# Seven block products for eight in the second pair of batches

## The chip, the cores and the metric

One core of a Trainium2 chip. The time is device microseconds of one execution; before the change the median of 3 runs is 703.04 us (702.79 to 703.9). The profile is of one further execution.

## The reference

Causal attention over 4 batches, 12 heads, 448 tokens, head dimension 64, then a gated product with no nonlinearity. Cut to what matters:

```python
scores = np.where(mask, -1e9, q @ k.T / 8)             # 4 x 12 x 448 x 448
attn = exp(scores - max) / (sum + 1e-9) @ v
x = attn laid out as (4 * 448) x 768
return ((x @ w_a) * (x @ w_b)) @ w_out                  # w_a, w_b: 768 x 1536, w_out: 1536 x 768
```

## The kernel before

Everything is held with features on the 128 partitions and the 448 tokens of one batch along the row. A weight unit is 128 output columns of a matrix with 768 input rows: 12 units of w_a ("a"), 12 of w_b ("b"), and 12 of w_out ("o", six output tiles, each in two halves of the 1536 inputs). One matmul takes 128 x 128 weights and 128 x 448 moving values into one PSUM bank; 6 k-tiles make a unit. Each fp32 operand is split into a high part, rounded to the format fp32r by a copy on ACT, and a low part, the rest, by a subtraction on DVE; a k-tile is three matmuls, hi by hi, hi by lo and lo by hi (`products`, L514). So a unit and batch is a group of 18 matmuls in one bank, and three banks "m" take turns.

The weights come as 64-bit words. DVE and ACT turn each unit into fp32 once (`convert_unit`, L297), and it is kept in HBM (`w_keep`).

The work has two passes over the same weights. Pass 1 takes batches 0 and 1, pass 2 batches 2 and 3. A pass is a list (`order`, L496): f = 0 to 5 with a then b, then six o units of the first half; f = 6 to 11, then six o units of the second half. `uses` (L549) walks it: for an a unit ACT copies the bank to SBUF ("mid"); for a b unit DVE multiplies bank and copy to g, and `part_g` splits g (g_hi by ACT, g_lo by DVE); an o unit reads g, and its first half goes to HBM (`o_keep`) and is added to the second. `split_unit` (L335) splits the weights of a unit ("w_hi", "w_lo", three buffers each).

The attention of batches 0 and 1 runs first. That of batches 2 and 3 is strewn into pass 1: `attend` (L594) counts k-tiles, and every 34 (`AT`) it puts in one pair of heads: scores, then in the next round the transposes and the product with v. The result x is stored in HBM (`x_keep`), and in the last six units of pass 1 `take_x` (L488) loads and splits it, 12 tiles, into the rooms that x of batches 0 and 1 has left.

All this only records operations with an engine, a cost and what they read and write. `Plan.order` (L125) then lists them: of the operations whose inputs are ready by its costs it takes the next for each engine, by age with some patience. The engines run what it wrote in that order, and semaphores hold an instruction until its inputs are there. Every DMA of the two passes is issued by SP, in one queue.

Of the kernel before, what the change touches and what calls it, by code (L numbers as in the profile page):

```python
# [9 lines left out]
F32 = mybir.dt.float32  # L10
# [31 lines left out]

AT = (2, 34)
STEP = (8, 3, 8)

PACE = (0, 0, 0, 0, 0, 0, 0, 0, 1, 0, 1, 0, 0)
LEAD = (2, 1)
# [170 lines left out]
def causal_attention_then_gated_product(  # L218
# [15 lines left out]
    def sb(tag, n, shape, dt=F32):  # L234
        return plan.ring(tag, n, lambda i: sbuf.tile(shape, dt, tag=f"{tag}{i}", name=f"{tag}{i}"))
# [13 lines left out]
    mask = const.tile([P, S], F32, name="mask")  # L249
    p_buf = [const.tile([P, PW], F32, name=f"p{i}") for i in range(NPB)]  # L250
    sm_buf = [const.tile([P, 2, 4], F32, name=f"sm{i}") for i in range(2)]
# [32 lines left out]

    w_64, w_32, w_parts = [], [], []

    def load_words(u):
# [3 lines left out]

    def load_kept(u):
        t = sb("w_32", 3, [P, UW])
        load(P * UW * 4, lambda: t.t, lambda: w_keep[u], [("keep", u)], [t])
        w_32.append(t)

    def convert_unit():  # L297
# [28 lines left out]
        w_32.append(wt)  # L326

    def split_unit():
        t = w_32.pop(0)
        hi, lo = sb("w_hi", 3, [P, KT, P], F32R), sb("w_lo", 3, [P, KT, P], F32R)  # L330

        def flat(x):
            return x.t.rearrange("p k f -> p (k f)")

        copy("act", UW, lambda: flat(hi), lambda: t.t, [t], [hi])  # L335
        two_input("dve", UW, lambda: flat(lo), lambda: t.t,
                  lambda: flat(hi).bitcast(F32), ALU.subtract, [t, hi], [lo])
        w_parts.append((hi, lo))


    qk, v_of, p_of, pt = {}, {}, {}, {}
    nth = [0, 0]

# [152 lines left out]
    order = []  # L496
    for _ in range(2):
# [4 lines left out]
    in_turn = [place[kind](n) for kind, n in order]  # L502
    xs, a_sb = {}, {}
# [9 lines left out]

    def products(ps, parts, k, hi, lo, first, last, keys):  # L514
        def mm():
            for n, (a, x) in enumerate(((parts[0], hi), (parts[0], lo), (parts[1], hi))):
                r = nc.tensor.matmul(  # L517
                    ps.t[:, :S], a.t[:, k, :], x(), start=first and n == 0, stop=last and n == 2
                )
            return r  # L520

        plan.op("pe", 3 * 203, mm, [parts[0], parts[1], *keys], [ps])

# [9 lines left out]
    def convert_next():  # L533
        n = turned[0]
        turned[0] += 1
        if n < NU:
            plan.soonest = HOLD[0] + HOLD[1] * n if n <= LEAD[0] else 0.0
            convert_unit()
            plan.soonest = 0.0
            load_next()  # L540
        elif n < len(in_turn):
            load_kept(in_turn[n])

    def split_next():
        if parted[0] < len(in_turn):
            split_unit()
        parted[0] += 1

    def uses():  # L549

        for n, (kind, f) in enumerate(order):
            first = n // NU * 2
            if n == NU - ET:
                for b in range(2, B):
                    xs[b] = x_parts()
            if NU - ET <= n < NU:
                for b in range(2, B):
                    take_x(b, xs[b], n - (NU - ET))
            convert_next()
            parts = w_parts.pop(0)  # L560
            split_next()
            for b in range(first, first + 2):
# [5 lines left out]
                for k in range(KT):  # L568
                    if kind == "o":
                        products(ps, parts, k, lambda k=k, b=b: g_hi[:, b % 2, k, :], lambda k=k, b=b: g_lo[:, b % 2, k, :],  # L570
                                 k == 0, k == KT - 1, [("g_hi", b % 2, k), ("g_lo", b % 2, k)])
                    else:
                        x_hi, x_lo = xs[b]
                        products(ps, parts, k, lambda k=k, x=x_hi: x.t[:, k, :], lambda k=k, x=x_lo: x.t[:, k, :],
                                 k == 0, k == KT - 1, [(x_hi, k), (x_lo, k)])
                    if k == KT - 1:
# [5 lines left out]
                        elif kind == "b":  # L582
                            two_input("dve", S, lambda t=t: t.t, lambda ps=ps: ps.t[:, :S],
                                      lambda a=a_sb[b]: a.t, ALU.mult, [ps, a_sb[b]], [t])
                            part_g(b, f, lambda t=t: t.t, t)
                        else:
                            two_input("dve", S, lambda t=t: t.t, lambda ps=ps: ps.t[:, :S],
                                      lambda a=acc: a.t, ALU.add, [ps, acc], [t])
                        if kind == "o":
# [112 lines left out]
```

## Time and profile before

| | us |
|---|---|
| median of 3 runs | 703.04 |
| profiled execution | 702.95 |
| its span, first to last instruction | 701.2 |
| PE busy | 690.3 |
| DVE busy | 391.3 |
| ACT busy | 341.6 |

The span has three parts: the attention of batches 0 and 1, up to some 102 us; pass 1 with the attention of batches 2 and 3, up to 438.1; pass 2, up to 697.3; then the last eviction and store. A busy time is the sum of instruction lengths with overlaps taken once. Matmuls overlap, so what one costs is read from the distance of two starts, and the same holds for DVE and ACT instructions where the queue is full.

### The profile page before, as it was taken

What the parts mean: (1) busy time and instruction counts of PE and PEld (TensorE: products, weight loads), DVE (VectorE), ACT (ScalarE), POOL (GpSimd) and SP (SyncE); (2) the same over time, 40 slices, a digit from 0 to 9 for tenths busy, and PEclk for the clock granted to TensorE, in tenths of its full rate; (3) what the DMA queues carried; (4) which work ended last, traced back from release to release, by engine and by line L of the source; (5) the groups of instructions that cost most, each with busy time, mean ns of one, the idle gap of its engine ahead of it and who ended that gap; (6) DMA issues with size and microseconds to landing.
All of it is one profiled execution on the core that took longest, in us unless ns stands there. A gap on an engine that the chain in (4) does not pass through costs nothing.

```text
span 701.2 us, 10638 instructions
## 1 busy us (share of the span) xinstructions
PE 690.3 (98%) x3884; PEld 598.8 (85%) x3884; DVE 391.3 (56%) x933; ACT 341.6 (49%) x817; POOL 56.2 (8%) x107
## 2 busy tenths in 40 slices
PE   8999999999999999999999999999999999999997
PEld 6665568898898898898898888999999999999997
DVE  6899998988876765777856543322331113322421
ACT  5778757667666667567566453222222222222100
POOL 4455650000000000000000000000000000000000
PEclk9999999999999999999999999999999999999999
DMA  8325535666655665443311566211214322121342
GB/s 313 117 86 164 147 120 175 228 195 224 205 206 188 224 218 182 153 154 145 141 66 51 189 195 190 63 65 46 67 46 148 122 87 67 45 68 46 97 133 92
DMA packets 41716, 95.85 MB, mean 137 GB/s; under 512 B 4800, under 2 KB 27840, under 8 KB 41664
## 3 DMA queue, kind: packets, MB, share of 16 engines
q1 hardware_dynamic: 41664, 95.18, 40.7%
q8 instruction: 30, 0.49, 0.3%
q14 instruction: 22, 0.18, 0.1%
HBM read 67.24 MB, written 27.92 MB: 136 GB/s over the span
## 4 chain that ended last, share of the span: by engine, by line
PE 90%; ACT 3%; DVE 3%; POOL 2%; DMA 1%; issue 1%; SPq 0%; POOLq 0%; ACTq 0%
PE m L517 74%; PE t L447 6%; PE s L379 5%; PE pv L467 4%; ACT p L398 2%; POOL p L425 2%; DVE p L392 1%; DMA raw<-kT 1%; ACT pt L263 1%; DVE rc L412 1%; PE m L379 1%; DVE pt L271 1%; SPq L282 0%; DVE w_m L312 0%; DVE rc L415 0%
## 5 line engine op out<-in xcount | busy, mean ns | idle before, releaser
L517 PE MATMUL m<-x_hi,w_hi 128*128 128x448 f32 x576 | 212.8, 369 | 0.0
L517 PE MATMUL m<-x_lo,w_hi 128*128 128x448 f32 x576 | 209.1, 363 | 0.0
L517 PE MATMUL m<-x_hi,w_lo 128*128 128x448 f32 x576 | 207.6, 360 | 0.0
L279 DVE TENSOR_TENSOR w_lo<-w,w_hi 128x768 fp32r<-128x768 f32 x72 | 69.0, 958 | 142.9 <-ACT w_hi L263 134.7
L517 PEld LDWEIGHTS m<-x_hi,w_hi 128*128 128x128 f32 x576 | 108.1, 188 | 11.3 <-issue 2.7
L398 ACT ACTIVATE p<-p,nm 128x448 f32<-128x448 f32 (+1 forms) x192 | 95.2, 498 | 43.0 <-DVE nm L392 42.8
L517 PEld LDWEIGHTS m<-x_hi,w_lo 128*128 128x128 f32 x576 | 107.7, 187 | 7.6
L517 PEld LDWEIGHTS m<-x_lo,w_hi 128*128 128x128 f32 x576 | 108.2, 188 | 5.3
L517 PE MATMUL m<-g_hi,w_hi 128*128 128x448 f32 x288 | 106.0, 368 | 0.0
L517 PE MATMUL m<-g_lo,w_hi 128*128 128x448 f32 x288 | 104.5, 363 | 0.0
L517 PE MATMUL m<-g_hi,w_lo 128*128 128x448 f32 x288 | 103.8, 360 | 0.0
L263 ACT ACTIVATE mid<-m 128x448 f32<-128x448 f32 x72 | 39.0, 541 | 123.5 <-PE m L517 112.9
L263 ACT ACTIVATE w_hi<-w 128x768 fp32r<-128x768 f32 x72 | 60.5, 840 | 55.2 <-PE m L517 54.9
L447 PE MATMUL t<-ident,p 128*128 128x128 f32 x384 | 64.4, 277 | 4.3 <-ACT pt L263 2.9
L392 DVE CUSTOM_DVE_ANT_0 p<-s,mask 128x448 f32<-128x448 f32 (+3 forms) x144 | 53.0, 414 | 25.7 <-PE s L379 25.6
L447 PEld LDWEIGHTS t<-ident,p 128*128 128x128 f32 x384 | 46.5, 140 | 14.1 <-POOL p L425 6.0
L517 PEld LDWEIGHTS m<-g_hi,w_hi 128*128 128x128 f32 x288 | 54.1, 188 | 5.0 <-issue 0.7
L517 PEld LDWEIGHTS m<-g_hi,w_lo 128*128 128x128 f32 x288 | 53.9, 187 | 3.9
L425 POOL TENSOR_SCALAR p<-p,rc 128x320 f32<-128x320 f32 (+2 forms) x96 | 53.2, 571 | 43.2 <-ACT p L398 26.1
L517 PEld LDWEIGHTS m<-g_lo,w_hi 128*128 128x128 f32 x288 | 54.1, 188 | 2.6
L263 ACT ACTIVATE pt<-t 128x512 f32<-128x512 f32 x72 | 41.2, 594 | 30.0 <-PE t L447 29.7
L279 DVE TENSOR_TENSOR mid<-m,mid 128x448 f32<-128x448 f32 x48 | 29.9, 624 | 46.4 <-PE m L517 46.1
(48 smaller groups left out, 655.6 us busy)
## 6 DMA issues: line engine op xcount, KB each, us to landing
w<-w SPq DMA_DIRECT2D x36, 768.0 KB, 4.5
w_keep<-w SPq DMA_DIRECT2D x36, 384.0 KB, 3.1
w<-w_keep SPq DMA_DIRECT2D x36, 384.0 KB, 3.0
raw<-qT SPq DMA_DIRECT2D x24, 224.0 KB, 2.7
raw<-kT SPq DMA_DIRECT2D x24, 224.0 KB, 3.1
o_keep<-mid SPq DMA_DIRECT2D x24, 224.0 KB, 1.9
acc<-o_keep SPq DMA_DIRECT2D x24, 224.0 KB, 2.7
out<-mid SPq DMA_DIRECT2D x24, 224.0 KB, 1.9
```

The costliest lines, as they stand in the source:

```text
L263: return nc.scalar.activation(o(), i(), AF.Copy)
L271: return nc.vector.tensor_copy(o(), i())
L279: plan.op(engine, ns, lambda: e.tensor_tensor(out=o(), in0=a(), in1=b(), op=op), reads, writes)
L379: r = nc.tensor.matmul(banks[j].t[:, at[i]], q[:, QS[i]:QS[i] + P], k[:, 0:QE[i]], start=True, stop=True)
L392: return nc.vector.tensor_tensor_reduce(out=chunk(p, i), in0=bk.t[:r, at[i]], in1=m, scale=-0.125, scalar=3.0e38, op0=ALU.add, op1=ALU.min ...
L398: return nc.scalar.activation(chunk(p, i), chunk(p, i), AF.Exp, bias=nm.t[:r, j, i:i + 1], scale=-1.0, accum_out=sm.t[:r, j, i:i + 1],)
L412: plan.op("dve", 69 + n, lambda sj=sj, si=si: nc.vector.tensor_scalar_add(rc.t[:, sj, si], sm.t[:, sj, si], 1.0e-9), [(sm, j, i) for j in ...
L425: return nc.gpsimd.tensor_scalar(out=pc, in0=pc, scalar1=s, scalar2=1.0, op0=ALU.mult, op1=ALU.mult)
L447: return nc.tensor.matmul(t.t[:, at:at + P], p.t[:, PO[i] + 128 * c:PO[i] + 128 * (c + 1)], swapped if swap else ident, is_transpose=True, ...
L467: r = nc.tensor.matmul(ps.t[j * D:(j + 1) * D, 128 * c:S], vt.t[:, c, j, :], parts[j, n].t[:, o:o + S - 128 * c], start=c == 0, stop=c == 3,)
L517: r = nc.tensor.matmul(ps.t[:, :S], a.t[:, k, :], x(), start=first and n == 0, stop=last and n == 2)
```

## The change

In pass 2 the two batches, x of batch 2 beside x of batch 3, and the two halves of the 768 inputs make a 2 x 2 of blocks B11, B12 (batch 3), B21, B22. For each f the a unit and the b unit are the two rows of a 2 x 2 of weight blocks, 384 x 128 each. The product of the two was 8 block products (4 groups of 18 matmuls); it is now 7 block products of 9 matmuls by Strassen's scheme in Winograd's form. An entry "s" takes the place of a and b in the list. The o units and pass 1 compute what they did.

- Weights: `prepare_all` makes S1 = b1 + b2, S2 = S1 - a1, S3 = a1 - b1, S4 = a2 - S2 on DVE (384 columns each), and splits the seven blocks one by one, four ahead of their use. `w_hi` and `w_lo` are one tile each of six half units.
- x: `take_first` and `take_second` load the 12 tiles, make T1 to T4 by 12 subtractions of 448 columns on DVE, and split the seven blocks, 21 splits. They begin five units before the end of pass 1. B11, B21, T1 and B22 lie in the old rooms of x, T2, T3 and T4 in buffers of the attention (p, pt) and of the 64-bit words (w_64).
- Products: `seven` runs them over three banks in the order B11 in bank A, T2 in B, B21 added in A, T3 added in B, T1 in C, T4 added in B, B22 added in C. ACT copies bank A after B11 (s1) and after B21 (c11). DVE adds s1 or an earlier sum to bank B or C after T2 (u2), T3 (u3), T1 (c22), T4 (c21) and B22 (c12); then c21 times c11 and c12 times c22 are g.
- `AT` is 30 instead of 34, so that the attention's rooms are free earlier.

```diff
-AT = (2, 34)
+AT = (2, 30)
+AHEAD = 4
+    w_hi = const.tile([P, 18, P], F32R, name="w_hi")
+    w_lo = const.tile([P, 18, P], F32R, name="w_lo")
...
+    def split(n, src, key, halves):
+        i = 3 * halves[0].tile
+        hi, lo = (x[:, i:i + n // P, :].rearrange("p k f -> p (k f)") for x in (w_hi, w_lo))
+        copy("act", n, lambda: hi, src, [key], [(h, 0) for h in halves])
+        two_input("dve", n, lambda: lo, src, lambda: hi.bitcast(F32), ALU.subtract,
+                  [key, *((h, 0) for h in halves)], [(h, 1) for h in halves])
...
-    def take_x(b, x, k):
-        t = sb("acc", 3, [P, S])
-        load(P * S * 4, lambda: t.t, lambda: x_keep[b - 2][k], [("xk", b, k)], [t])
-        split_x(x, k, lambda: t.t, t, False)
+    def take_first(k):
+        one, two = (sb("raw", 4, [P, 2, S]) for _ in range(2))
...
+        for t, i, b, kk in ((one, 0, 2, k), (one, 1, 3, k), (two, 1, 3, k + 3), (two, 0, 2, k + 3)):
+            load(P * S * 4, lambda t=t, i=i: t.t[:, i], lambda b=b, kk=kk: x_keep[b - 2][kk], [("xk", b, kk)], [(t, i)])
+        split_block("B11", k, b11, (one, 0))
+        both(b11, b12, b11, ALU.subtract, [(one, 1)], [(one, 0)])
+        split_block("T1", k, b11, (one, 0))
+        both(b12, b22, b12, ALU.subtract, [(two, 1)], [(one, 1)])
+        split_block("B22", k, b22, (two, 1))
+        both(b22, b22, b11, ALU.subtract, [(one, 0)], [(two, 1)])
+        split_block("T2", k, b22, (two, 1))
+        split_block("B21", k, b21, (two, 0))
+    def take_second(k):
+        one, two = raw_x[k]
+        split_block("T3", k, lambda: one.t[:, 1], (one, 1))
+        both(lambda: two.t[:, 0], lambda: two.t[:, 0], lambda: two.t[:, 1], ALU.subtract, [(two, 1)], [(two, 0)])
+        split_block("T4", k, lambda: two.t[:, 0], (two, 0))
...
-            order += [("ab"[r], f) for f in range(h * HF, (h + 1) * HF) for r in range(2)]
+            for f in range(h * HF, (h + 1) * HF):
+                order += [("a", f), ("b", f)] if r == 0 else [("s", f)]
...
+    def prepare_all(f0):
+        for f in range(f0, f0 + HF):
+            a, b = weights[f]
+            for i in range(7):
+                if i in (0, 4):
+                    if f + 1 < f0 + HF:
+                        weights.setdefault(f + 1, []).append(load_32(place["ab"[i // 4]](f + 1)))
...
+                if i == 1:
+                    sub(s12, lower, b, lower, b, upper, ALU.add)
+                    sub(s12, upper, s12, lower, a, lower)
+                if i == 3:
+                    sub(s34, lower, a, lower, b, lower)
+                    sub(s34, upper, a, upper, s12, upper)
+                t, at = ((a, lower), (s12, upper), (a, upper), (s34, lower), (s12, lower), (b, upper), (s34, upper))[i]
+                h = half()
+                split(384, lambda t=t, at=at: t.t[:, at], t if t in (a, b) else (t, at.start), [h])
+                ready.append(h)
+                yield
+    def seven(f, n):
+        bank_a, bank_b, bank_c = (bank("m", 3) for _ in range(3))
...
+        plan_of = ((bank_a, "B11", True), (bank_b, "T2", True), (bank_a, "B21", False), (bank_b, "T3", False),
+                   (bank_c, "T1", True), (bank_b, "T4", False), (bank_c, "B22", False))
+        for i, (ps, name, first) in enumerate(plan_of):
+            next(to_prepare[0], None)
...
+            w = ready.pop(0)
+            for k in range(3):
+                (hi, hi_key), (lo, lo_key) = (part[k] for part in block[name])
+                products(ps, w, k, hi, lo, first and k == 0, k == 2, [hi_key, lo_key], True)
...
+            if n == NU - 5:
+                make_rooms()
+                take_first(0)
+            elif n == NU - 4:
+                take_first(1)
+            elif n == NU - 3:
+                more_rooms()
+                take_second(0)
+                take_first(2)
+            elif n == NU - 2:
+                take_second(1)
+            elif n == NU - 1:
+                take_second(2)
```

Of DVE before, one f of pass 2: mid is the product of a bank "m" and a copied a, g_lo and w_lo are the low parts of g and of a unit.

```order
L279 TENSOR_TENSOR w_lo1_4911<-w_321_4768,w_hi1_4906 128x768 [waits DMAHW3_49,PE_49,Activation_49]
L279 TENSOR_TENSOR mid4_4928<-m1_4897,mid2_4880 128x448 [waits DMAHW0_49,PE_49]
L279 TENSOR_TENSOR g_lo_78<-mid4_4928,g_hi_77 128x448 [waits Activation_49]
L279 TENSOR_TENSOR mid0_4951<-m2_4924,mid3_4901 128x448 [waits PE_49]
L279 TENSOR_TENSOR w_lo2_4959<-w_322_4819,w_hi2_4953 128x768 [waits DMAHW4_49,Activation_49]
L279 TENSOR_TENSOR g_lo_78<-mid0_4951,g_hi_77 128x448 [waits Activation_49]
```

Of DVE now, nine instructions of pass 2 around the end of one f: the first is c12's eviction, the last u2 of the next f; w_e_s holds the sums S1 and S2, w_m_s S3 and S4.

```order
L284 TENSOR_TENSOR mid3_4837<-m2_4776,acc2_4770 128x448 [waits PE_49]
L284 TENSOR_TENSOR w_e_s1_4844<-w_321_4810 128x384 [waits DMAHW3_49]
L284 TENSOR_TENSOR mid3_4837<-mid3_4837,mid1_4807 128x448 [waits DVE_49]
L284 TENSOR_TENSOR g_lo_80<-mid2_4822,g_hi_79 128x448 [waits Activation_49]
L284 TENSOR_TENSOR w_lo_73<-w_322_4694,w_hi_72 128x384
L284 TENSOR_TENSOR g_lo_80<-mid3_4837,g_hi_79 128x448 [waits Activation_49]
L284 TENSOR_TENSOR w_e_s1_4844<-w_e_s1_4844,w_320_4741 128x384 [waits DMAHW2_49]
L284 TENSOR_TENSOR w_lo_73<-w_m_s0_4759,w_hi_72 128x384 [waits PE_49,Activation_49]
L284 TENSOR_TENSOR acc1_4878<-m1_4851,mid4_4860 128x448 [waits PE_49]
```

Six DVE instructions for each f have become twenty, and a sum that waits for a load now stands between an eviction and the next.

Of PE now, in the same f as that u2: the last matmul of T2 in bank m1, the ends of B21 in bank m0, and the first matmuls of T3, whose moving operands lie in the rooms w_64.

```order
L584 MATMUL m1_4851<-pt_x0_4441,w_lo_73 128x448
L584 MATMUL m0_4833<-x_hi0_4161,w_hi_72 128x448 [waits Activation_49]
L584 MATMUL m0_4833<-x_lo0_4172,w_hi_72 128x448
L584 MATMUL m0_4833<-x_hi0_4161,w_lo_73 128x448
...
L584 MATMUL m1_4851<-w_64_x1_4217,w_hi_72 128x448 [waits DVE_49]
L584 MATMUL m1_4851<-w_64_x2_4323,w_hi_72 128x448
L584 MATMUL m1_4851<-w_64_x1_4217,w_lo_73 128x448
```

PE comes back to bank m1 after one group of 9 matmuls, where before 36 matmuls in the two other banks stood between two uses of a bank, and the first matmul of the return waits for DVE's u2.

## Rows read from the trace of the kernel before

**Rows 1.** The page: span, busy time, and PE in 40 slices (tenths).
```profile
span 701.2 us, 10638 instructions
PE 690.3 (98%) x3884; PEld 598.8 (85%) x3884; DVE 391.3 (56%) x933; ACT 341.6 (49%) x817; POOL 56.2 (8%) x107
PE   8999999999999999999999999999999999999997
```
**Rows 2.** The chain of waits from 430.3 us on: start us, us, what.
```profile
430.26 267.22 PE m L517 x1335
697.49 0.02 issue
697.51 0.63 DVE mid L279
```
**Rows 3.** Pass 2 by stretches: PE, PEld, DVE, ACT, POOL busy (x), PEclk, DMA share, GB/s.
```profile
438.10:524.50 86.40, 86.40 (x433) 80.98 (x433) 25.71 (x36) 22.20 (x35) 0.00 (x0) 1.00 0.19 58
524.50:567.70 43.20, 43.20 (x217) 40.49 (x217) 6.92 (x8) 11.05 (x18) 0.00 (x0) 1.00 0.39 130
567.70:654.10 86.40, 86.40 (x433) 80.98 (x433) 24.83 (x34) 22.62 (x36) 0.00 (x0) 1.00 0.18 58
654.10:697.30 43.20, 43.20 (x217) 40.30 (x216) 11.87 (x17) 3.93 (x5) 0.00 (x0) 1.00 0.36 116
```
**Rows 4.** Instructions by time where a group ends: start, us, engine, line [idle before].
```profile
448.71 0.36 PE L517 MATMUL m<-x_hi,w_lo 128*128 128x448 f32 x1
448.91 0.36 PE L517 MATMUL m<-x_hi,w_hi 128*128 128x448 f32 x1
449.11 0.62 DVE L279 TENSOR_TENSOR mid<-m,mid 128x448 f32<-128x448 f32 x1 [1.28 <-PE m L517]
```
**Rows 5.** DVE's instructions by time in a full stretch of pass 1.
```profile
112.06 0.62 DVE L279 TENSOR_TENSOR mid<-m,mid 128x448 f32<-128x448 f32 x1
112.60 0.95 DVE L317 SCALAR_TENSOR_TENSOR w_m<-w_m,w 128x768 f32<-128x768 uint32 x1
...
116.41 0.94 DVE L279 TENSOR_TENSOR w_lo<-w,w_hi 128x768 fp32r<-128x768 f32 x1
117.28 0.55 DVE L310 TENSOR_SCALAR w_e<-w 128x768 uint32<-128x768 uint32 x1
```
**Rows 6.** A wait of PE for ACT in the first attention, by time.
```profile
44.15 0.58 ACT L263 ACTIVATE pt<-t 128x512 f32<-128x512 f32 x1
...
44.78 0.66 PE L447 MATMUL t<-ident,p 128*128 128x128 f32 x4 [0.92 <-ACT pt L263]
```
**Rows 7.** Groups of instructions, 438 to 524.5 us: busy us, mean ns | idle before.
```profile
L517 PEld LDWEIGHTS m<-x_hi,w_hi 128*128 128x128 f32 x144 | 27.0, 188 | 2.2
...
L279 DVE TENSOR_TENSOR w_lo<-w,w_hi 128x768 fp32r<-128x768 f32 x12 | 11.5, 958 | 39.2 <-ACT w_hi L263 38.6
L263 ACT ACTIVATE w_hi<-w 128x768 fp32r<-128x768 f32 x12 | 10.1, 842 | 11.3 <-PE m L517 11.3
L279 DVE TENSOR_TENSOR mid<-m,mid 128x448 f32<-128x448 f32 x11 | 6.9, 625 | 16.2 <-PE m L517 16.2
...
L263 ACT ACTIVATE mid<-m 128x448 f32<-128x448 f32 x12 | 6.5, 545 | 33.4 <-PE m L517 33.4
L263 ACT ACTIVATE g_hi<-mid 128x448 fp32r<-128x448 f32 x11 | 6.4, 579 | 17.5 <-DVE mid L279 17.5
```
**Rows 8.** Tile w_keep, 440 to 697 us: loads of kept weights.
```profile
L282 SPq DMA_DIRECT2D w<-w_keep x31: 319/319/973, 440.0 to 656.0; - x31
...
DMA to landing us min/median/max: 2.7/2.9/3.6
```
**Rows 9.** Tile x_keep, 400 to 440 us.
```profile
DMA to landing us min/median/max: 2.4/4.1/5.1
```
**Rows 10.** Normalisation of one pair on ACT, and its transposes in the chain.
```profile
194.46 3.29 ACT L424 ACTIVATE p<-p,rc 128x448 f32<-128x448 f32 x8
...
206.49 1.09 PE t L447 x10
```
**Rows 11.** Pass 1 with attention, as rows 3.
```profile
140.00:430.00 290.00, 290.00 (x1651) 252.07 (x1651) 197.08 (x410) 181.13 (x422) 0.00 (x0) 1.00 0.50 171
```

More of the change, by code (lines that the diff above doesn't have):

```diff
@@ L486, in split_x, with places @@
                   [key, (x_hi, k)], [(x_lo, k)])
-    def take_x(b, x, k):
-        t = sb("acc", 3, [P, S])
-        load(P * S * 4, lambda: t.t, lambda: x_keep[b - 2][k], [("xk", b, k)], [t])
-        split_x(x, k, lambda: t.t, t, False)
+    block = {}
+    def places(tag, n, take, count, width):
+        t = plan.ring(tag, n, lambda i: sbuf.tile([P, width], F32R, tag=f"{tag}{i}", name=f"{tag}_x{i}"))
+        return [((lambda c=c: t.t[:, SHIFT + c * S:SHIFT + (c + 1) * S]), (t, c)) for c in range(take)]
@@ new lines, in make_rooms @@
+    def make_rooms():
+        for b, (lower, upper) in ((2, ("B11", "B21")), (3, ("T1", "B22"))):
+            hi, lo = x_parts()
+            for n, name in enumerate((lower, upper)):
+                block[name] = [[((lambda x=x, k=3 * n + k: x.t[:, k, :]), (x, 3 * n + k)) for k in range(3)]
+                               for x in (hi, lo)]
+        block["T2"] = [[*places("p", 3, 2, 2, PW), *places("pt", 6, 1, 1, 512)] for _ in range(2)]
+        block["T4"] = [[*places("p", 3, 2, 2, PW), *places("pt", 6, 1, 1, 512)]]
@@ new lines, in more_rooms, with split_block, both @@
+    def more_rooms():
+        block["T4"].append(places("w_64", 3, 3, 3, 2 * UW))
+        block["T3"] = [places("w_64", 3, 3, 3, 2 * UW) for _ in range(2)]
+    def split_block(name, k, i, key):
+        (hi, hi_key), (lo, lo_key) = (part[k] for part in block[name])
+        copy("act", S, hi, i, [key], [hi_key])
+        two_input("dve", S, lo, i, lambda: hi().bitcast(F32), ALU.subtract, [key, hi_key], [lo_key])
+    raw_x = {}
+    def both(o, a, b, op, reads, writes):
+        two_input("dve", S, o, a, b, op, reads, writes)
@@ L500, in causal_attention_then_gated_product @@
             order += [("o", 2 * e + h) for e in range(ET)]
     place = {"a": lambda n: 2 * n, "b": lambda n: 2 * n + 1, "o": lambda n: NA + n}
-    in_turn = [place[kind](n) for kind, n in order]
+    in_turn = [place[kind](n) if kind in place else None for kind, n in order]
     xs, a_sb = {}, {}
@@ L512, in part_g, with products @@
                   lambda: g_hi[:, b, f, :].bitcast(F32), ALU.subtract, [key, ("g_hi", b, f)], [("g_lo", b, f)])
-    def products(ps, parts, k, hi, lo, first, last, keys):
+    def products(ps, w, k, hi, lo, first, last, keys, part=False):
         def mm():
-            for n, (a, x) in enumerate(((parts[0], hi), (parts[0], lo), (parts[1], hi))):
+            i = 3 * w.tile + k
+            for n, (a, x) in enumerate(((w_hi, hi), (w_hi, lo), (w_lo, hi))):
                 r = nc.tensor.matmul(
-                    ps.t[:, :S], a.t[:, k, :], x(), start=first and n == 0, stop=last and n == 2
+                    ps.t[:, :S], a[:, i, :], x(), start=first and n == 0, stop=last and n == 2, skip_group_check=part
                 )
             return r
-        plan.op("pe", 3 * 203, mm, [parts[0], parts[1], *keys], [ps])
+        plan.op("pe", 3 * 200, mm, [(w, 0), (w, 1), *keys], [ps])
     to_load = iter(in_turn[:NU])
@@ L540, in convert_next @@
             load_next()
-        elif n < len(in_turn):
-            load_kept(in_turn[n])
+        elif n < len(order):
+            kind, f = order[n]
+            if kind == "s" and f % HF == 0:
+                weights[f] = [load_32(place["a"](f)), load_32(place["b"](f))]
+                to_prepare[0] = prepare_all(f)
+            elif kind == "o" and f >= 4:
+                load_kept(in_turn[n])
     def split_next():
-        if parted[0] < len(in_turn):
-            split_unit()
+        n = parted[0]
@@ L573, in uses @@
                         x_hi, x_lo = xs[b]
[L574 removed]
+                        products(ps, parts[k // 3], k % 3, lambda k=k, x=x_hi: x.t[:, k, :], lambda k=k, x=x_lo: x.t[:, k, :],
                                  k == 0, k == KT - 1, [(x_hi, k), (x_lo, k)])
```

102 lines of the change are left out of this document (79 added, 23 removed).

## The prediction

> **What bounds the kernel now.** I read the page first, then the chain of waits, then the second pass by stretches, then single instructions. The page has PE busy in 690.3 of 701.2 us and 9 tenths or more in every slice from the second to the last but one [rows 1]. A busy PE is not yet a PE at its peak, so the chain decides: from 430.26 us to the end it is one piece, 1335 matmuls in 267.22 us, then the last eviction [rows 2]; 267.22 / 1335 = 0.200 us each. The second pass runs from 438.1 to 697.3, 259.2 us for its 36 units x 2 batches x 18 = 1296 matmuls, again 0.200, in four stretches of 86.4, 43.2, 86.4 and 43.2 us [rows 3]. A matmul starts 0.20 us after the one before, across the end of a group too [rows 4]. So the pass is matmul count times 0.200 us, at a granted clock of 1.00 (the 2.4 GHz level), while DVE is busy in 25.7 of 86.4 us and ACT in 22.2 [rows 3]. Only a change in the number of matmuls, or a new wait of PE, moves the end.
>
> **Removed.** In pass 2 the uses of a and b take 24 units x 36 = 864 matmuls. Seven products of 3 k-tiles x 3 matmuls are 63 for each f; 12 of them are 756. The order of the changed kernel has 3124 PE rows against 3232. 108 matmuls x 0.200 us = 21.6 us, all on the path that sets the end. Each stretch of 86.4 us becomes 6 x 63 x 0.200 = 75.6 us. Moving operands from x and from g both run at 0.200 [rows 3]; T2, T3 and T4 move out of other rooms, 27 of the 63, which no row shows. I take 0.200 for them: below it stands the weight load, 0.188 us of PEld for each matmul [rows 7], which bounds a gain at 12 x 27 x 0.012 = 3.9 us; no row of this shape starts later than 0.200, so nothing bounds a loss but the rivals.
>
> **Added on DVE in the block stretch.** One f had two w_lo, two products and two g_lo. It now has 7 w_lo and 4 sums of 384 columns, 5 evictions that add, 2 products, 2 g_lo: 20 instructions. What one costs in a full queue is the distance of starts: 0.54 us for 448 columns (112.06 to 112.60), 0.87 for 768 (116.41 to 117.28) [rows 5]. No instruction of 384 is in the trace; on the line through these two it takes 0.474. So 11 x 0.474 + 9 x 0.54 = 10.1 us of an f of 12.6 us: 80%, against 30% before. ACT: durations 0.842 for 768 and 0.579 for 448 [rows 7] give 0.53 for 384, so 7 x 0.53 + 2 x 0.545 + 2 x 0.579 = 6.0 us. Both fit. What decides is whether single results come in time.
>
> **The new waits of PE.** A group was 18 matmuls and came back to its bank after two other groups, 7.2 us. Now a group is 9 matmuls, 1.8 us, and PE returns to a bank with one group between in four places of each f: bank A at B21, B at T3 and T4, C at B22 (48 returns in all). An eviction starts 0.20 us after the next group's first matmul (448.91 and 449.11) [rows 4] and takes 0.625 us [rows 7]. PE goes on 0.05 us after the engine ends (44.15 + 0.58 = 44.73, PE at 44.78; that is ACT, and I take it for DVE) [rows 6]. Together 0.87 of 1.80 us, so a return is hidden until the eviction stands 0.93 us in its queue.
>
> The worst place is u2, since eight DVE instructions stand between c12 of the f before and u2. Count from the start of an f. c12 can start at 0.20; then in the changed order a sum, a product, g_lo, w_lo, g_lo, a sum, w_lo follow. Starts: 0.20, 0.74, 1.21, 1.75, 2.29, 2.77, 3.31, 3.78; u2 at 4.25 instead of 3.80, done at 4.87, bank B free at 4.92. T3 wants it at 5.40: 0.48 us to spare. The second g_lo waits for ACT, which gets the product at 1.21 + 0.63 = 1.84 and needs 0.58: 2.42, before 2.77. s1 on ACT stands behind that g_hi: it ends near 3.0, and bank A is wanted at 3.60. u3, c22 and c21 find DVE free. In four of the twelve f's the planner puts 3 matmuls of T1 ahead of T3, which gives T3 0.6 us more and takes 0.6 from T4; u3 starts at 8.0, is done at 8.63, bank B free at 8.68, wanted at 9.0. So no wait: I take 0. From the other side: if each DVE instruction held its queue for its whole duration (0.625 for 448, 0.958 for 768 [rows 7], so 0.557 for 384), u2 would start at 0.20 + 4 x 0.625 + 4 x 0.557 = 4.93, bank B is free at 5.60, 0.20 us late; in the eight f's without T1 ahead that is 8 x 0.20 = 1.6 us.
>
> **Weights by sums.** a and b come back in the number they did (two per f). The load of the next b may start when its buffer's last w_lo is read, near 8.5 us of an f, and its sum stands behind c21's product, at 12.5 at the earliest. A load takes 2.7 to 3.6 us [rows 8]: it lands by 12.1, 0.4 us to spare. Behind that sum wait c12, its product and in the end u2. If it lands after 5.1 us, the longest that a load of x_keep took [rows 9], the sum is 1.1 us late and u2, with 0.48 to spare, misses T3 by 0.6: 8 x 0.6 = 5 us at worst. I take 0, by the loads of the same tile.
>
> **End of pass 1.** Reading x back took 12 splits; it takes 21 now and 12 subtractions. From the eviction of the last b unit's first batch to the first block product, 71 DVE instructions stand: 49 of 448 columns, 15 of 384 and 7 of 768, so 49 x 0.54 + 15 x 0.474 + 7 x 0.87 = 40 us, beside 13 groups x 3.6 us and some 4 us of attention on PE, 51 us. The queue is full for the first 20 us of it; an output group has 7.2 us until its bank is wanted, so some 6 us of DMA waits cost nothing. Loads of x_keep land in 2.4 to 5.1 us [rows 9], most are issued several units early: 0, with an upper end of a few us.
>
> **Attention 30 steps apart instead of 34.** PE has no idle time in that stretch (290.00 busy of 290.00) [rows 11], and the same instructions stay. The transposes come 4 x 0.6 = 2.4 us earlier after their scores. The probabilities are done at 197.75 and transposed at 206.49 [rows 10]: 8.7 us become 6.3. 0; without that cover each of 12 pairs would cost what is missing. Wider const tiles for w, other rooms, and the flag on the matmuls change no instruction's length that a row shows: 0.
>
> **Sum.** The profiled execution took 702.95 us, its span 701.2 and 1.75 around it; the median of the runs is 703.04. 702.95 - 21.6 = 681.35; with the median 0.1 higher, 681.4 us.
>
> **Rivals.**
> 1. DVE is late at bank B. A DVE instruction then holds its queue for its whole duration: 11.7 us of 12.6, and 1.6 us of PE waits as above: 683.0. Against it stand the starts 0.54 apart of instructions 0.62 long [rows 5]; for it, that most of these instructions wait on a semaphore, which those rows mostly don't. The Trainium skill, VectorE: DVE Perf Modes, section "The DRAIN you can't avoid", says that the next operation does not start until the pipe is empty; read strictly this is that rival, and the trace's 0.54 after 0.62 speaks for an overlap.
> 2. The b loads are late and u2 misses T3 behind them: up to 5 us, 686.4. For it: 0.4 us to spare. Against: 31 loads of this tile, none over 3.6 us [rows 8].
> 3. Slower: DVE stands still for the loads of x_keep at the end of pass 1. Twelve loads, each waited for in full at the median 4.1 us, are 49 us on a queue with 40 us of work; 6 are free, so 681.4 + 43 = 724. It is slower than before once the waits pass 6 + 21.6 = 27.6 us, 2.3 us for each load. For it: the raw buffers are four, and the last two are loaded only when their earlier blocks are split. Against: only 4 of the 12 loads are of that kind, which makes 16 us and 691.
> 4. That it doesn't do what it says is out: the PE rows are 108 fewer.
>
> **How the numbers follow.** Forecast, PE streaming throughout, 681.4 (680.8 to 682.8): 0.70. Rival 1: 0.14. Rival 2, or a few us at the change of passes: 0.11. Rival 3: 0.05, of which about 0.02 near no change. A measurement of this kernel tells 0.2%, 1.4 us, from no change. Range 679.8 to 687.5: it holds the forecast, rival 1, rival 2 to its full price and a part of the gain from cheaper matmuls. Faster 0.95, same 0.02, slower 0.03.
>
> **What would show it.** Right: the block stretches are 75.6 us each, every matmul 0.200 after the one before, DVE about 80% busy there, PE with no idle at bank returns, the first output group of pass 2 75.6 us after the first block product. Rival 1 shows gaps of 0.1 to 0.3 us before T3 that DVE ends; rival 2 the same gaps with DMA ahead of DVE's sums; rival 3 a gap of PE between the last b unit and the first block product. Matmuls out of the new rooms at another distance than 0.200 would make the first term wrong.

## The result, and the profile after

The changed kernel takes 682.71 us (median of 4 runs, 682.41 to 683.08), the kernel before in the same session 702.92 (702.79 to 703.90): ratio 0.971, 95% interval 0.9693 to 0.9727. The forecast was 681.4. So the change brings 20.2 us, where 21.6 were forecast. By the time alone, rival 1 (683.0) lies nearer than the forecast; the traces below decide between the two.

The page of the changed kernel, against [rows 1]: 20.3 us less span and 108 matmuls less, PE as full as before.

```profile
span 680.9 us, 10745 instructions
PE 670.2 (98%) x3776; PEld 578.6 (85%) x3776; DVE 475.5 (70%) x1122; ACT 365.7 (54%) x886; POOL 56.2 (8%) x107
PE   8999999999999999999999999999999999999997
```

Its chain of waits from 401 us on, against [rows 2]: again one piece of matmuls to the end and one eviction behind it. No wait of PE stands in it.

```profile
401.73 275.46 PE m L584 x1371
677.19 0.02 issue
677.22 0.62 DVE mid L284
```

But 275.46 / 1371 is 0.2009 us for each matmul, not 0.200. The excess sits in the blocks of pass 2. Here is that pass by stretches, cut where PE goes from blocks to output groups and back (columns as in [rows 3]).

```profile
438.38:514.50 76.12, 76.12 (x380) 70.93 (x378) 56.66 (x106) 31.29 (x62) 0.00 (x0) 1.00 0.21 67
514.50:557.70 43.20, 43.20 (x218) 40.49 (x216) 12.88 (x21) 12.21 (x22) 0.00 (x0) 1.00 0.31 111
557.70:633.82 76.12, 76.12 (x380) 70.93 (x378) 56.12 (x105) 31.72 (x63) 0.00 (x0) 1.00 0.23 73
633.82:677.00 43.18, 43.18 (x217) 40.31 (x215) 12.85 (x19) 4.15 (x6) 0.00 (x0) 1.00 0.39 129
```

The output stretches are what they were, 43.2 us. The two block stretches are 76.12 us each instead of the forecast 75.6, with PE busy all the time at a granted clock of 1.00 (the 2.4 GHz level): 0.52 too much, twice. PE does not wait there; its matmuls stand further apart. PE by time in the second f of the first block stretch (a row with x2 is two matmuls):

```profile
452.67 0.36 PE L584 MATMUL m<-x_hi,w_lo 128*128 128x448 f32 x1
452.86 0.57 PE L584 MATMUL m<-p_x,w_hi 128*128 128x448 f32 x2
453.28 0.37 PE L584 MATMUL m<-p_x,w_lo 128*128 128x448 f32 x1
453.48 0.57 PE L584 MATMUL m<-p_x,w_hi 128*128 128x448 f32 x2
...
454.09 0.57 PE L584 MATMUL m<-pt_x,w_hi 128*128 128x448 f32 x2
...
454.70 0.36 PE L584 MATMUL m<-x_hi,w_hi 128*128 128x448 f32 x1
```

Three matmuls that move p_x take 453.48 - 452.86 = 0.62 us, the three that move pt_x 454.70 - 454.09 = 0.61. T2 moves out of p and pt, T3 out of w_64 (w_x in the rows), T4's high part out of p and pt and its low part out of w_64. Over any four matmuls in a row that move out of one room (5th to 95th percentile from the last attention on, first start to fourth, so three distances): x and g 600 ns, as before the change; p_x 613 to 618; w_64 602 to 614. Of pt only three stand in a row: in T2 they take 610 to the start of the next.

The last 0.2 us lie ahead of both passes: the first product starts at 89.43 us instead of 89.20. Over the fourteen profiled executions of this study that start lies anywhere from 88.92 to 90.85, whatever was edited. So the experiments below are read by the distance from the start of the first product (the first matmul with a weight unit) to that of the last, which doesn't contain it.

### The profile page after: what moved, and what is told of

Same layout as the page of the kernel before. It is cut to its first block, busy times and chain, and to the rows that moved or that the text cites. A ratio compares the mean times of both kernels' runs of the same rounds, so it can differ in the third digit from the quotient of the medians.

```text
span 680.9 us, 10745 instructions
## 1 busy us (share of the span) xinstructions
PE 670.2 (98%) x3776; PEld 578.6 (85%) x3776; DVE 475.5 (70%) x1122; ACT 365.7 (54%) x886; POOL 56.2 (8%) x107
## 4 chain that ended last, share of the span: by engine, by line
PE 91%; ACT 3%; DVE 3%; POOL 2%; issue 1%; POOLq 0%; ACTq 0%
PE m L584 73%; PE t L463 6%; PE s L395 5%; PE pv L483 4%; ACT p L414 2%; POOL p L441 2%; DVE p L408 1%; PE fill L814 1%; ACT pt L268 1%; PE m L395 1%; DVE rc L428 1%; DVE pt L276 1%; DVE w_m L321 0%; DVE rc L431 0%; POOLq L868 0%
## 5 line engine op out<-in xcount | busy, mean ns | idle before, releaser
L584 PE MATMUL m<-x_hi,w_hi 128*128 128x448 f32 x432 | 161.1, 373 | 0.0
L584 PE MATMUL m<-x_lo,w_hi 128*128 128x448 f32 x432 | 156.8, 363 | 0.0
L584 PE MATMUL m<-x_hi,w_lo 128*128 128x448 f32 x432 | 155.9, 361 | 0.0
L284 DVE TENSOR_TENSOR w_lo<-w,w_hi 128x768 fp32r<-128x768 f32 (+1 forms) x84 | 65.8, 783 | 53.4 <-ACT w_hi L268 52.7
L268 ACT ACTIVATE w_hi<-w 128x768 fp32r<-128x768 f32 (+1 forms) x84 | 59.1, 704 | 69.0 <-PE m L584 55.7
L584 PEld LDWEIGHTS m<-x_hi,w_hi 128*128 128x128 f32 x432 | 81.1, 188 | 9.3 <-issue 3.0
L584 PEld LDWEIGHTS m<-x_hi,w_lo 128*128 128x128 f32 x432 | 80.8, 187 | 5.7
L584 PEld LDWEIGHTS m<-x_lo,w_hi 128*128 128x128 f32 x432 | 81.2, 188 | 4.1
L284 DVE TENSOR_TENSOR mid<-m,acc 128x448 f32<-128x448 f32 x48 | 29.9, 624 | 45.3 <-PE m L584 44.8
```

The costliest lines, as they stand in the source:

```text
L268: return nc.scalar.activation(o(), i(), AF.Copy)
L284: plan.op(engine, ns, lambda: e.tensor_tensor(out=o(), in0=a(), in1=b(), op=op), reads, writes)
L584: r = nc.tensor.matmul(ps.t[:, :S], a[:, i, :], x(), start=first and n == 0, stop=last and n == 2, skip_group_check=part)
```

## The experiments

Two questions. First, why are the matmuls out of the new rooms longer? Theory P: the address at which the moving rows start sets the spacing. In the built kernels the tiles of x and pt lie at multiples of 256 bytes and their blocks begin 64 bytes in; g lies at 64 modulo 256; the rooms p and w_64 lie at 128 modulo 256, so that their blocks begin at 192. (These places are those of the built programs; a trace does not show addresses, only the steps of 64, 128 and 256 bytes below are in the edits. The expectations call w_64 the 64 KB room; 64 stands for the 64-bit words.) A block row is 1792 bytes, 7 x 256, so all blocks of a tile begin alike. Rival R: it is the rooms, or hi and lo out of several tiles. Second, were the covers that the prediction took to hide everything else really there, and how large? A cover is the time by which a result is ready before it is wanted.

All fourteen profiled executions, in us:

| kernel | first product | last product | distance | time |
|---|---|---|---|---|
| before | 89.20 | 697.11 | 607.91 | 702.95 |
| changed | 89.43 | 676.82 | 587.39 | 682.70 |
| after_again | 89.23 | 676.62 | 587.39 | 682.53 |
| rooms64 | 89.41 | 675.76 | 586.35 | 681.59 |
| s48 | 88.92 | 678.43 | 589.51 | 684.25 |
| s0 | 89.58 | 681.07 | 591.50 | 686.91 |
| lo256 | 89.78 | 677.17 | 587.39 | 683.01 |
| dve1 | 89.83 | 677.63 | 587.80 | 683.46 |
| dve2 | 89.72 | 680.62 | 590.90 | 686.46 |
| dve3 | 89.29 | 685.45 | 596.16 | 691.28 |
| bload2 | 90.68 | 678.06 | 587.38 | 683.61 |
| btwice | 89.71 | 677.10 | 587.39 | 682.79 |
| xtwice | 90.85 | 678.23 | 587.38 | 683.79 |
| at30 | 89.82 | 697.76 | 607.95 | 703.71 |

**rooms64 and after_again.** The blocks in the rooms p and w_64 128 bytes further on, and the changed kernel once more beside it.

```diff
-        return [((lambda c=c: t.t[:, SHIFT + c * S:SHIFT + (c + 1) * S]), (t, c)) for c in range(take)]
+        at = SHIFT + (0 if tag == "pt" else 32)
+        return [((lambda c=c: t.t[:, at + c * S:at + (c + 1) * S]), (t, c)) for c in range(take)]
```

> The changed kernel with one edit: the blocks that lie in the old p rooms and in the 64 KB room (w_64) begin 32 floats, 128 bytes, further on in them, so that their rows start at 64 modulo 256 bytes like those of x and g; in the changed kernel they start at 192. Nothing else differs: the same instructions in the same order. Seen so far: in the changed kernel three matmuls that move x or g take 600 ns from start to start, three that move p_x about 616, those of w_64 about 614, and the two block stretches of pass 2 take 76.12 us each, where 12 times 63 matmuls at 0.200 make 75.6. Theory P (the start of the moving rows sets the spacing): all triples come to 600 ns, the block stretches to 75.6 us each, the time to 682.7 - 2 x 0.52 = 681.7 us. Rival R (it is the rooms themselves, or hi and lo from several tiles, wherever the rows start): triples of p and w_64 stay at 614 to 616 ns and the time at 682.7. Rival W (the DVE or a bank's return holds the matmuls back by some ns): no change either, 682.7.

> The changed kernel unchanged, to be compared on one chip with the kernel in which the blocks start elsewhere. Expected by every theory: 682.7 us as before, 20.2 us below the kernel before, with block stretches of 76.1 us.

On one chip: rooms64 681.85 us (681.36 to 682.26), ratio to the kernel before 0.9691 (0.9678 to 0.9704); the changed kernel 682.57 (681.87 to 683.38), 0.9703 (0.9689 to 0.9716). The intervals overlap, as they must for 0.15%. The traces are sharper. The same f as above, PE by time in rooms64: the same three matmuls of p take 453.36 - 452.76 = 0.60, those of pt 454.56 - 453.96 = 0.60.

```profile
452.56 0.36 PE L585 MATMUL m<-x_hi,w_lo 128*128 128x448 f32 x1
452.76 0.56 PE L585 MATMUL m<-p_x,w_hi 128*128 128x448 f32 x2
453.16 0.36 PE L585 MATMUL m<-p_x,w_lo 128*128 128x448 f32 x1
453.36 0.56 PE L585 MATMUL m<-p_x,w_hi 128*128 128x448 f32 x2
...
453.96 0.56 PE L585 MATMUL m<-pt_x,w_hi 128*128 128x448 f32 x2
...
454.56 0.36 PE L585 MATMUL m<-x_hi,w_hi 128*128 128x448 f32 x1
```

Its block stretches are the forecast 75.60 us to the last digit:

```profile
438.36:513.96 75.60, 75.60 (x380) 70.88 (x378) 56.63 (x106) 31.26 (x62) 0.00 (x0) 1.00 0.23 68
...
557.16:632.76 75.60, 75.60 (x380) 70.88 (x379) 56.10 (x105) 31.69 (x63) 0.00 (x0) 1.00 0.24 73
```

Every three matmuls out of p, pt and w_64 now take 600 ns; first to last product is 1.04 us shorter, the shortest distance of the study. R and every explanation by DVE or banks fall: the rooms, the order and the waits were the same. One thing P does not say: pt did not move, its rows start at 64 in both kernels, and yet its three matmuls in T2 went from 610 to 600. They stand right behind those of p, so what runs beside a matmul has a part in its spacing too. How, is not shown: in T4 pt's three, also behind p but with w_64 as the low part between them, take 601 in the changed kernel.

**s48 and s0.** The same question from the other side: all blocks moved, by SHIFT.

```diff
-SHIFT, LINE = 16, 64
+SHIFT, LINE = 48, 64      # s48
+SHIFT, LINE = 0, 64       # s0
```

> The changed kernel with SHIFT = 48 for 16: every block starts 128 bytes further on in its tile, so that x and g rows start at 192 modulo 256 bytes, those of p and of the 64 KB room at 64. Theory P (the start of the rows sets the spacing) turns the picture round: triples that move x or g take some 614 to 616 ns in both passes, those of p and w_64 600 ns; some 2,650 matmuls move x or g after the attention (of 3,100, 448 columns each), each about 5 ns longer, so the time goes up by 10 to 14 us, to about 693 to 697. Rival R (the rooms themselves): p and w_64 stay at 614 to 616, x and g at 600, 682.7 us. What starts at 64 also says whether the o stretches of pass 2 (43.2 us now) move: P 44.2, R 43.2.

> The changed kernel with SHIFT = 0: every block starts 64 bytes earlier in its tile, so that rows of x and pt start at 0 modulo 256 bytes, those of p and of the 64 KB room at 128, g at 64 as before. The result is as before. Seen so far: 64 gives 600 ns for three matmuls whatever the room (x, g, p, w_64), 192 gives 614 to 618 for p, 602 to 614 for w_64 and 604 to 608 for x. Theory P (the start of the moving rows modulo 256 bytes sets the spacing, the room does not): x triples come to one value and p and w_64 to one, neither seen before, and what 0 and 128 are worth is read off; 600 for both would give 681.6 us, as with all rooms at 64. If every start but 64 costs about 6 ns for three matmuls, x included, some 1.5 to 2 us over 682.7, as with SHIFT = 48, which took 684.25.

Chains from the last attention on: the 1371 matmuls that took 275.46 us in the changed kernel take more in both. s48 first, then s0:

```profile
402.92 275.88 PE m L584 x1371
```

```profile
403.83 277.62 PE m L584 x1371
```

Three distances in one room as above, in ns, by where the rows start modulo 256 bytes:

| start | x | g | p_x | w_64 |
|---|---|---|---|---|
| 64 | 600 (changed, rooms64) | 600 (all runs) | 600 (rooms64), 600 to 604 (s48) | 600 (rooms64), 600 to 612 (s48) |
| 192 | 602 to 608 (s48) | | 613 to 618 (changed) | 602 to 614 (changed) |
| 0 | 604 to 620 (s0) | | | |
| 128 | | | 605 to 615 (s0) | 605 to 613 (s0) |

The direction is P's: x becomes slow as soon as it leaves 64, p fast when it comes there, and g, which no SHIFT moves, stays at 600. A mere change between starts is not the cause: in the a and b units of pass 1 of s48, where x follows x, three matmuls take 604 to 607. In s48 the rows at 64 are not quite at 600 everywhere: the first three matmuls out of w_64, behind x, take 612 or 613 in eleven of the twelve f's, the next two threes 600 each.

The size that I expected of s48, 10 to 14 us, was wrong twice. I counted g and more: 1296 matmuls move x, 432 threes. And x at 192 costs some 6 ns for three, not the 15 of p. Between first and last product s48 lost 2.12 us: some 1.7 by x in pass 1 and 0.81 by x in pass 2, and 0.23 by pt, which is now at 192, while p and w_64 gave back 0.63.

Nor do room and start together set the size. In s0 block B11, the same rows each time, opens the first f behind g and the second f behind B22. PE by time, first matmul of B11 and first of T2, in the first f and in the second:

```profile
440.47 0.36 PE L584 MATMUL m<-x_hi,w_hi 128*128 128x448 f32 x1
...
442.30 0.36 PE L584 MATMUL m<-p_x,w_hi 128*128 128x448 f32 x1
```

```profile
453.30 0.37 PE L584 MATMUL m<-x_hi,w_hi 128*128 128x448 f32 x1
...
455.16 0.36 PE L584 MATMUL m<-p_x,w_hi 128*128 128x448 f32 x1
```

The nine matmuls take 1.83 us and then 1.86: 608, 604 and 611 ns for each three, then 620 three times.

**lo256.** Why p at 192 costs 15 ns and x at 192 only 6: are hi and lo alike modulo 512 the reason?

```diff
-        block["T2"] = [[*places("p", 3, 2, 2, PW), *places("pt", 6, 1, 1, 512)] for _ in range(2)]
+        block["T2"] = [[*places("p", 3, 2, 2, PW, more), *places("pt", 6, 1, 1, 512)] for more in (0, 64)]
...
-        block["T3"] = [places("w_64", 3, 3, 3, 2 * UW) for _ in range(2)]
+        block["T3"] = [places("w_64", 3, 3, 3, 2 * UW, more) for more in (0, 64)]
```

> The changed kernel with the lo blocks in the p rooms and the 64 KB room 256 bytes further on in their tiles; hi stays. All still start at 192 modulo 256 bytes. The result is as before. With SHIFT = 48, x at 192 modulo 256 came to 604 to 608 for three matmuls, p in the changed kernel to 614 to 618. One difference is read from the addresses of the built kernels: there x_hi and x_lo stand 256 bytes apart modulo 512, here p's hi and lo stand alike. Theory Q (hi and lo alike modulo 512 is what makes the slow ones slowest): p triples fall from 615 to about 606, w_64 to 604 to 607, the block stretches from 76.12 to about 75.9 us, the time to about 682.2. Theory P alone (only modulo 256 counts): nothing changes, 615 and 607, 76.12, 682.7. All at 600 would say that the distance of hi and lo decides, and not the start.

No: p_x 613 to 618 and w_64 602 to 614 as in the changed kernel, first to last product 587.39 in both. A step of 128 bytes counts, and this one of 256 in the low rows does not. What sets the size at one start is left open; by s0 and pt above, the matmuls beside them have a part in it.

**dve1, dve2, dve3.** How much cover do the bank returns have? One, two or three useless sums of 448 columns behind c12's eviction.

```diff
-                added(c12, bank_c, u2)
+                def late(c12=c12, bank_c=bank_c, u2=u2):
+                    r = nc.vector.tensor_tensor(out=c12.t, in0=bank_c.t[:, :S], in1=u2.t, op=ALU.add)
+                    for j in range(1):    # 2, 3
+                        nc.vector.tensor_tensor(out=v_buf[j].rearrange("p a b d -> p (a b d)")[:, :S], in0=mask, in1=mask, op=ALU.add)
+                    return r
+                plan.op("dve", dve_ns(S), late, [bank_c, u2], [c12])
```

> The changed kernel with one more DVE instruction in every f of the block stretches: a sum of 448 columns (mask + mask into an old v buffer, read by nobody) right behind c12's eviction. The result is as before. In the trace of the changed kernel u2 ends 0.60 us before the first T3 matmul in the worst f's (two of six in each stretch), 0.82 in one, 0.99 in two, and 0.97 in the first, which has no c12 before it; PE goes on 0.05 after an eviction ends. Theory A, the prediction's account (the chain from c12 to u2 moves by one start distance, 0.54): the worst cover of 0.55 just holds it, no PE wait, 682.7 us (span 680.9). Theory B (a DVE instruction that waits takes its whole duration, so 0.62 or more): 4 f's late by some 0.1, 683.1. Theory C (the returns have far more cover than read): nothing here and nothing with two or three.

> As with one more sum behind c12, now with two, 1.08 us. Theory A: 1.08 - 0.55 = 0.53 late at T3 in 4 f's, 1.08 - 0.77 = 0.31 in 2, 1.08 - 0.94 = 0.14 in 4: 3.3 us of PE waits that DVE ends, all in the block stretches, so about 686.0 us. Theory B: 1.25 in place of 1.08, 5.0 us, 687.7. Theory C: 682.7.

> As before with three sums behind c12, 1.62 us. Theory A: 1.07 late in 4 f's, 0.85 in 2, 0.68 in 4: 8.7 us, about 691.4 us; DVE then holds 23 instructions for each f, 11.7 of 12.7 us. Theory B: 1.87 in place of 1.62, 11.2 us, 693.9. Theory C: 682.7. If the wait at T3 also delays T4 or the next f's u2, more than Theory A says.

First to last product grows by 0.41, 3.51 and 8.77 us; A said 0, 3.3 and 8.7, B 0.4, 5.0 and 11.2, C nothing. So the cover is about what the trace showed, and used up by one more instruction. dve1's 0.41 is B's number, but not for B's reason: the queue moves by A's 0.54 each. u2 of the third f starts 4.22 us into the f in the changed kernel, 4.76, 5.29 and 5.83 with one, two and three more. But A had the place only half right. In the third f of dve2 (first product 464.28) PE waits 0.36 us at B21, for bank A, ahead of T3. ACT by time, then PE:

```profile
467.21 0.58 ACT L268 ACTIVATE g_hi<-mid 128x448 fp32r<-128x448 f32 x1 [1.94 <-DVE mid L284]
467.70 0.53 ACT L268 ACTIVATE mid<-m 128x448 f32<-128x448 f32 x1
```

```profile
467.72 0.37 PE L584 MATMUL m<-pt_x,w_lo 128*128 128x448 f32 x1
468.28 0.47 PE L584 MATMUL m<-x_hi,w_hi 128*128 128x448 f32 x1 [0.19 <-ACT mid L268]
468.59 0.37 PE L584 MATMUL m<-x_lo,w_hi 128*128 128x448 f32 x1
...
469.99 0.37 PE L584 MATMUL m<-x_hi,w_lo 128*128 128x448 f32 x1
470.25 0.68 PE L584 MATMUL m<-w_x,w_hi 128*128 128x448 f32 x2
```

The late product of DVE holds g_hi on ACT, s1 stands behind it, and s1 empties bank A. T3 (m<-w_x at 470.25) is then only 0.06 late. And each wait costs some 0.11 us beside its own length, since the matmul after the waiting one is late as well: 468.59 - 468.28 = 0.31. That is also all of dve1's loss: one gap of 0.28 to 0.30 us, at the second matmul of T3, in each of 4 f's. That A's sums came so near is in part luck: it had left out these 0.11 us and the wait at B21, and in dve2 it counted 0.31 in the last f of each stretch, where PE does not wait.

**bload2 and btwice.** Rival 2, the late load of b: first with two copies in DRAM meant to delay it, then with the load itself made twice.

```diff
-                        weights.setdefault(f + 1, []).append(load_32(place["ab"[i // 4]](f + 1)))
+                        u = place["ab"[i // 4]](f + 1)                                  # bload2
+                        t = sb("w_32", 3, [P, UW])
+
+                        def loads(u=u, t=t, more=2 * (i == 4)):
+                            for j in range(more):
+                                nc.sync.dma_start(out=spare[f0 // HF][j], in_=w_keep[u])
+                            return nc.sync.dma_start(out=t.t, in_=w_keep[u])
...
```

```diff
-                        weights.setdefault(f + 1, []).append(load_32(place["ab"[i // 4]](f + 1)))
+                        u = place["ab"[i // 4]](f + 1)                                  # btwice
+                        t = load_32(u)
+                        if i == 4:
+                            load(P * UW * 4, lambda t=t: t.t, lambda u=u: w_keep[u], [("keep", u)], [t])
+                        weights.setdefault(f + 1, []).append(t)
```

> The changed kernel with two more DMAs on SP's queue right ahead of each later load of b in the block stretches (ten loads): the same 384 KB of w_keep copied to a spare place in DRAM. The result is as before. In the trace of the changed kernel such a load is issued about 4.2 us before the DVE sum that reads it and lands after 2.8 to 3.0, so it has some 1.2 us to spare; the prediction's own estimate was 0.4. Two copies ahead should make it land 2 to 5 us later, by the 2.7 us that one load takes and what of it overlaps. Theory A (rival 2's mechanism: the sum waits, u2 behind it misses T3): the sum is 1 to 4 us late, T3 0.5 to 3 us late in ten f's, 5 to 30 us in all, 688 to 712, with PE waits that DVE ends at T3 and DVE waits that the load of w ends. Theory C (loads have more cover than that, or the copies do not delay them): 682.7.

> The changed kernel with each later load of b in the block stretches (ten) made twice into the same buffer, the second DMA waiting for the first; the result is as before. So b lands some 3.3 us later (one more landing of 3.0 and an issue of 0.3). In the trace of the changed kernel the load of b is issued 4.0 to 4.3 us before the DVE sum that reads it and lands after 3.0: 1.0 to 1.2 us to spare. Theory A (rival 2's mechanism: the sum waits, u2 stands behind it on DVE and misses T3): the sum is 2.1 to 2.3 us late, T3 late by that less its cover of 0.55, 0.77 or 0.94: about 1.6 in 4 f's, 1.4 in 2, 1.25 in 4, 14 us in all, so about 697 us, with DVE's waits for w<-w_keep 2 us each ahead of PE's. Theory C (the loads have more cover than that, DVE catches up before u2): 682.7 to 686.

Both 587.4 us from first to last product: nothing lost. bload2 tells nothing on the rival: the copies went out some 5 to 7 us ahead of b's load, behind the load of a, and b landed after 2.7 to 3.2 us as always. btwice does delay it, and Theory A's 14 us did not come, for a reason that it had left out: the planner counts the second load and puts the sum that reads b behind u2. DVE by time in the second f of btwice (first product 451.34):

```profile
455.34 0.62 DVE L284 TENSOR_TENSOR acc<-m,mid 128x448 f32<-128x448 f32 x1
455.88 0.55 DVE L284 TENSOR_TENSOR w_lo<-w,w_hi 128x384 fp32r<-128x384 f32 x1
456.34 0.55 DVE L284 TENSOR_TENSOR w_e_s<-w 128x384 f32<-128x384 f32 x1
```

The sum (w_e_s<-w) stands at 5.0 us of the f, where in the changed kernel it comes within 0.74 us of an f's start, and still costs PE nothing. So a load of b that the planner expects late was harmless here. One that comes late against the plan, the rival's own case, was not produced by either run. Nor did it come by itself: in the ten profiled executions of the seven-product kernel that leave these loads alone, the 80 loads of b whose sum falls into a block stretch landed in 2.7 to 3.5 us.

**xtwice.** Rival 3, the reading back of x at the end of pass 1: every load twice, the second waiting for the first.

```diff
-            load(P * S * 4, lambda t=t, i=i: t.t[:, i], lambda b=b, kk=kk: x_keep[b - 2][kk], [("xk", b, kk)], [(t, i)])
+            for _ in range(2):
+                load(P * S * 4, lambda t=t, i=i: t.t[:, i], lambda b=b, kk=kk: x_keep[b - 2][kk], [("xk", b, kk)], [(t, i)])
```

> The changed kernel with each of the twelve loads of x_keep at the end of pass 1 made twice into the same place, the second waiting for the first; the result is as before. Each then lands some 2.5 to 3.5 us later. Theory A (the trace of the changed kernel: the last block piece is written at 418.24 us, the first block product starts at 438.38, so the reading back has 20 us of cover, not the 6 us that rival 3 was priced with): no PE wait, 682.7 us, and the last piece written some 5 to 12 us later. Rival 3 as priced (6 us free, each load waited for): 12 x 3 - 6 = 30 us more, 713; for the four loads that wait for buffers alone 4 x 3 - 6 = 6 us, 689.

No PE wait, 587.38 us. The last block piece, on DVE in the changed kernel and then in xtwice:

```profile
417.62 0.62 DVE L284 TENSOR_TENSOR w_x<-raw,pt_x 128x448 fp32r<-128x448 f32 x1
```

```profile
424.55 0.62 DVE L284 TENSOR_TENSOR w_x<-raw,pt_x 128x448 fp32r<-128x448 f32 x1
```

It comes 6.9 us later (1.4 of them by the later start of the whole), and the first block product (438.38 there, 439.79 here) doesn't notice: 20.1 us of cover in the changed kernel, 14.6 left here. The time of 683.79 is the late first product (90.85).

**at30.** The kernel before with AT = (2, 30) alone.

```diff
-AT = (2, 34)
+AT = (2, 30)
```

> The kernel before with one number of the change alone: AT = (2, 30) for (2, 34), so that the attention of the second pair is set off four steps earlier and nothing else changes. The prediction costs this part at nothing. If so, 702.9 us as before. If the shorter cover at the end of pass 1 costs something, or the earlier start gives something (the changed kernel begins its products at 89.43 us instead of 89.20 and each pass at its own time), the time differs by that: the start of pass 2 then lies off 438.11 us by as much, and the rest of the trace is as before.

703.78 us against 703.47, ratio 1.0004 (0.9995 to 1.0013), first to last product 607.95 against 607.91: nothing, as expected.

## Why the prediction was right, and where it was not

**Removed matmuls: right in number, wrong by 1.04 us in price.** The term that came out too small rests on "T2, T3 and T4 move out of other rooms ... I take 0.200 for them ... nothing bounds a loss but the rivals". These 27 of the 63 matmuls of an f do stand further apart than 0.200: 1.00 us over 12 x 27 = 324 matmuls, 3.1 ns each, and 0.04 in the three of x right behind T3. The cause shown is where the rows of p and w_64 start (192 where x and pt have 64). With rows that start where those of x do, the term is what was forecast: 607.91 - 586.35 = 21.56 of 21.6 us (rooms64). The prediction named this itself as what would make the first term wrong, but gave it no price; I had priced only the gain that the weight load (0.188) bounds.

**The rest of the miss, 0.2 us,** is the start of the first product, which scatters by up to 1.9 us between executions.

**DVE's queue and the bank returns: right.** DVE by time in the third f of the changed kernel (first product 463.75):

```profile
463.95 0.62 DVE L284 TENSOR_TENSOR mid<-m,acc 128x448 f32<-128x448 f32 x1 [0.17 <-PE m L584]
464.49 0.55 DVE L284 TENSOR_TENSOR w_e_s<-w 128x384 f32<-128x384 f32 x1
464.96 0.62 DVE L284 TENSOR_TENSOR mid<-mid,mid 128x448 f32<-128x448 f32 x1
465.49 0.62 DVE L284 TENSOR_TENSOR g_lo<-mid,g_hi 128x448 fp32r<-128x448 f32 x1
466.03 0.55 DVE L284 TENSOR_TENSOR w_lo<-w,w_hi 128x384 fp32r<-128x384 f32 x1
...
467.97 0.62 DVE L284 TENSOR_TENSOR acc<-m,mid 128x448 f32<-128x448 f32 x1
```

Instructions of 384 columns are 0.47 apart (464.49 to 464.96), as the line through [rows 5] gave (0.474), and last 0.55; those of 448 are 0.53 to 0.54 apart. u2 (acc) starts 467.97 - 463.75 = 4.22 us into the f, forecast 4.25. Beside it ACT's s1 and PE's first matmuls of B21 and of T3, by time:

```profile
466.09 0.53 ACT L268 ACTIVATE mid<-m 128x448 f32<-128x448 f32 x1
...
467.39 0.36 PE L584 MATMUL m<-x_hi,w_hi 128*128 128x448 f32 x1
...
469.19 0.57 PE L584 MATMUL m<-w_x,w_hi 128*128 128x448 f32 x2
```

T3 starts 0.60 us after u2's end (467.97 + 0.62): 0.55 to spare by the 0.05 of [rows 6], forecast 0.48. B21 wants bank A at 467.39, and s1 ends at 466.62: 0.72 to spare with the 0.05 off, where the prediction's numbers give 0.55. DVE's share is lower than the 80% said: 56.66 of 76.12 us, 74%, since of 120 instructions only 106 fall in the stretch; the others are done before and after it.

**Rival 1 is out.** DVE instructions that had to wait do not hold the queue for their whole duration: the starts above are 0.47 and 0.53 apart for 0.55 and 0.62 long ones, and three more sums move u2 by 3 x 0.54. The strict reading of the sentence in the Trainium skill (VectorE: DVE Perf Modes, "The DRAIN you can't avoid") is not what these rows show; the section itself goes on to say that a next operation that is not held starts earlier, as these do. The rival's place was right, though: one more instruction there and PE begins to wait. At two more, bank A behind ACT comes before bank B.

**Rivals 2 and 3 did not occur,** and I had both too near. Loads of w_keep landed in 2.7 to 5.0 us, median 2.9, in pass 2; b's load is issued 4.0 to 4.3 us ahead of its sum, forecast 4.0 (8.5 and 12.5 us into the f), and lands in 2.7 to 3.0: 1.1 to 1.5 to spare, where my 0.4 took the longest landing of [rows 8], 3.6. The two slow loads, 4.4 and 5.0, are of a. That b got none of them is not explained here; by these figures a b load of 5.0 would have made its sum 0.7 to 0.9 us late. DVE has no wait for a load in the block stretches. The end of pass 1 had 20.1 us of cover where I had 11 (51 - 40) and 6 of DMA waits.

**Attention 30 steps apart and the rest at nothing: right** (at30, and 43.20 us for the first output stretch).

## What to carry to other kernels

When PE is the bound and streams, a change in the number of matmuls is worth their count times the spacing, and the spacing can depend on where the moving rows start: check a new room's start address against one whose spacing the trace shows before taking the spacing over. Where a group shrinks, write the queue behind each bank return from start distances, not from durations, through every engine that stands in it (here DVE, then ACT); 0.5 us of cover for a 12.6 us loop was enough, and one more instruction was not. And read a small difference between two points that the edit encloses: here first to last product repeated within 0.01 us where whole times scatter by more than 1.

## What the runs showed of the hardware that was not expected

Three matmuls of 448 columns take 600 ns from start to start when all moving rows start at 64 modulo 256 bytes (rooms64: x, g, p, pt and w_64 alike), and 602 to 620 out of rows at 0, 128 and 192, at a granted clock of 1.00 throughout. The size hangs on what runs beside them as well: rows at 64 took 610 behind rows at 192 (pt in T2 of the changed kernel), and the same rows of x at 0 took 604 to 611 in one f and 620 in the next (s0). Why, no run here settles. A matmul behind one that had to wait starts 0.31 us after it instead of 0.20 (dve2, dve3), so a wait of PE costs 0.1 us more than its length.
